# Turning q and k by ordinary products with the identity, placed between the score products of a slot

## The chip, the cores and the metric

The kernel runs on one core of a Trainium2 chip. The metric is device time in microseconds (us). TensorE (PE in the profile) does the matrix products, and its weight loads have records of their own (PEld). VectorE is DVE, ScalarE is ACT, GpSimd is POOL, and SyncE (SP) issues most of the transfers.

## The reference, cut to what matters

Attention over 2 batches, 8 heads, 768 tokens and 64 dimensions per head, then two MLPs over the 1536 tokens. A query sees the keys whose hash agrees with its own: six bits, the signs of products with `proj`.

```python
q_bits = (np.einsum('bhsd,dk->bhsk', q, proj) > 0)
k_bits = (np.einsum('bhsd,dk->bhsk', k, proj) > 0)
mask = q_bucket[:, :, :, None] == k_bucket[:, :, None, :]
scores = np.where(mask, scale * np.matmul(q, k.transpose(0, 1, 3, 2)), -1e9)
attn = np.exp(scores - np.max(scores, axis=-1, keepdims=True))
attn = attn / (np.sum(attn, axis=-1, keepdims=True) + 1e-09)
x = np.matmul(attn, v)                       # heads side by side: 1536 x 512
x = (silu(x @ w_gate) * (x @ w_val)) @ w_out
x = layernorm(solu(x @ w_in)) * g_ln @ w_out2
```

## The kernel before, in words

The attention works on eight pairs of heads. A pair is 12 slots; a slot is 128 queries of one head against all 768 keys. Slots are numbered `i` over the whole stage, and `l` is the slot's place in its pair `p`. Everything is written out by hand inside `manual_schedule()`: each engine runs its instructions in the order in which the loop at L819 issues them.

float32 values are kept as two parts, a rounded high one and the rest, both in the type fp32r (a float32 that TensorE multiplies in one pass). `parts[p, "q"]` and `parts[p, "k"]` hold both parts of a token side by side, 128 values on the free axis. The score products want them with these values on the partitions, so each block of 128 tokens is turned on TensorE: 12 blocks for each head (6 of k, 6 of q), four at a time into one PSUM bank. One such group of four is a *turn* (`turns`, L460): four transposes (L475), the fourth of them with its type read as float32, and after a `yield` one or two ScalarE copies out of the bank (L480; L482 and L483; or L492), and transfers that put the pieces where the scores read them. A head takes three turns, `g` = 0, 1, 2.

A slot issues, in this order:

- DVE takes the row maxima of the slot's scores (`maxima`, L563).
- PE transposes the exponentials of two slots earlier, two groups of three blocks of 128x128 (`transposes`, L597 and L595). In a slot without a turn the last of the six is read as float32 (L595); in a slot with a turn it is not.
- `go(work)` at L836: PE does the four transposes of a turn, if the slot has one (`turning`, L728, says which: l = 0, 1, 3, 9, 10, 11 in most pairs), or hash products (L514) in other slots. In the first pair `beginning` (L756) plays this part, with one or two turns at a time.
- PE computes the scores of the next slot (`scores`, L544): two products with the high parts (`ka`, `qa`) and two with the low parts and hash bits (`kb`, `qb`), each of 384 columns, into one of two score tiles. The tile is that of the slot before, so the first of the four waits for that slot's exponential.
- ACT and DVE take the transposed exponentials out of PSUM (`highs` L606, `lows` L610).
- PE multiplies the values of a head, four products (`values`, L632, L636, L631).
- `go(work)` at L851: the ACT copies of the turn.
- ACT computes the slot's exponential (`exps`, L577), with the row sums read out after it (ACTIVATION_READ_ACCUMULATOR).

After the attention the two MLPs run from L870 on, as products of 512 columns without pause; nothing of them is changed.

Of the kernel before, what the change touches and what calls it, by code (L numbers as in the profile page):

```python
# [10 lines left out]
F32 = mybir.dt.float32  # L11
R32 = mybir.dt.float32r
# [9 lines left out]
P = 128  # L22
# [49 lines left out]
def hash_attention_then_two_mlps(  # L72
# [16 lines left out]
    nc = tc.nc  # L89
# [46 lines left out]
    first = {}  # L136
# [41 lines left out]
    for g in range(4):  # L178
        m = (g + 1) % 2
# [50 lines left out]
    with at:  # L230
# [6 lines left out]
        ps_a = at.enter_context(tc.tile_pool(name="ps_a", bufs=1, space=PSUM))  # L237
        ps_p = at.enter_context(tc.tile_pool(name="ps_p", bufs=1, space=PSUM))
# [68 lines left out]
        def move(dst, src):  # L307
            nc.sync.dma_start(dst.bitcast(F32), src.bitcast(F32))
# [137 lines left out]
        def tiles_of_head():  # L446
            return {
                x: (kp if x == "kt" else ab).tile([P, S], R32, tag=x, name=x)
                for x in ("qa", "qb", "ka", "kb", "kt")
            }  # L450
# [3 lines left out]
        def turn(p, j, g, bank=None):  # L454

            return turns(p, j, g, bank) if p < len(pairs) else iter(())

        def turns(p, j, g, bank):  # L460

            if (p, j) not in turned:
                turned[p, j] = tiles_of_head()
            x = turned[p, j]
            if bank is None:
                t = ps_p.tile([P, 512], R32, tag="pp", name="pp")
            else:
                t = ps_a.tile([P, 512], R32, tag="av", name="av")
            for m in range(4):
                nm, c = ("k", 4 * g + m) if 4 * g + m < C else ("q", 4 * g + m - C)  # L470
                sides = (
                    t[:, m * P:(m + 1) * P],
                    parts[p, nm][:, j, c].rearrange("p t d -> p (t d)"), idr,
                )
                nc.tensor.transpose(*(x.bitcast(F32) if m == 3 else x for x in sides))  # L475
            yield
            t = t.bitcast(F32)
            qa, qb, ka, kb, kt = (x[nm] for nm in ("qa", "qb", "ka", "kb", "kt"))
            if g == 0:
                nc.scalar.mul(kt[:, 0:512], t, qscale)  # L480
            elif g == 1:
                nc.scalar.mul(kt[:, 512:S], t[:, 0:S - 512], qscale)  # L482
                nc.scalar.copy(qa[:, 0:1024 - S], t[:, S - 512:512])  # L483
                move(qb[D:P], kt[0:D])
                keys = [(ka[0:D], kt[0:D]), (ka[D:P], kt[0:D]), (kb[0:D], kt[D:P])]
                if p == 1:
                    held.extend(keys)
                else:
                    for dst, src in keys:
                        move(dst, src)  # L490
            else:
                nc.scalar.copy(qa[:, 1024 - S:S], t)  # L492
                move(qb[0:D], qa[0:D])
                if p == 1 and j == 1:
                    for dst, src in held:
                        move(dst, src)
# [37 lines left out]
        def quarter(h):  # L534


            p, l = divmod(h, 4)
            return (p, l // 2, l % 2) if p == 0 else (p, l % 2, l // 2)
# [2 lines left out]

            return quarter(h)[1] == 1

        def scores(i):  # L544
            if not 0 <= i < NSLOT:
                return
            p, j, n = quarter(i // CH)
            x, c = turned[p, j], n * CH + i % CH
            s = s_tiles[i % 2]
            rows = slice(c * P, (c + 1) * P)  # L550
            for a, m, first in ((x["qa"], x["ka"], True), (x["qb"][:MB], x["kb"][:MB], False)):
                for n in range(2):
                    nc.tensor.matmul(  # L553
                        s[:, n, :HALF], a[:, rows], m[:, n * HALF:(n + 1) * HALF],
                        start=first, stop=not first,
                    )
            s_of[i] = s

        def maxima(i):
# [23 lines left out]
        def transposes(i, g, last=False):  # L583
            if not 0 <= i < NSLOT:
                return
            h, c = divmod(i, CH)
            if c == 0 and g == 0:
                eh_of[h] = et.tile([P, C, HALF], R32, tag="eh", name="eh")
                el_of[h] = et.tile([P, C, HALF], R32, tag="el", name="el")
            t = ps_t.tile([P, CH, P], R32, tag="t", name="t")  # L590
            e, moved = e_of[i]
            for m in range(CH):
                cols = slice(m * P, (m + 1) * P)
                if last and m == CH - 1:
                    nc.tensor.transpose(t.bitcast(F32)[:, m, :], e[:, g, cols], idf)  # L595
                else:
                    nc.tensor.transpose(t[:, m, :], moved[:, g, cols], idr)  # L597
            t_of[i, g] = t.bitcast(F32)
# [5 lines left out]
        def highs(i, g):  # L604
            if 0 <= i < NSLOT:
                nc.scalar.copy(half_tile(eh_of, i, g), t_of[i, g])  # L606
# [115 lines left out]
        def go(work):  # L722

            next(work, None)
# [31 lines left out]
        def beginning(i):  # L756

            at = {
                3: lambda: (turn(1, 0, 0), turn(1, 0, 1, 1)),
                4: lambda: (turn(1, 0, 2), turn(1, 1, 0, 1)),  # L760
                5: lambda: (turn(1, 1, 1),),
                6: lambda: (turn(1, 1, 2),),
                8: lambda: (hashes(1, 0, False),),
                9: lambda: (hashes(1, 1, False),),
                10: lambda: (turn(2, 0, 0),),
                11: lambda: (turn(2, 0, 1),),
            }
            works = at[i]() if i in at else ()
            for work in works:
                go(work)  # L770
            yield
            for work in works:
                go(work)
# [34 lines left out]
        with tc.manual_schedule():  # L808
            for p, nm in ((1, "k"), (1, "q"), (0, "v")):
                load(p, nm)  # L810
            first_weights = early()
            opening = (
                step for of in ((1, "k"), (1, "q"), (0, "v")) for step in split_heads(*of)
            )
            opened = start()
            hashed = next(opened)
            done = leaving = iter(())
            splits = {}
            for i in range(NSLOT + 9):  # L819
                p, l = divmod(i, SLOTS)  # L820
                h, part = divmod(i - 5, CH)
                if i < SLOTS:
                    work = beginning(i)
                else:
                    work = turning(p, l)
                if part == 0:
                    leaving, done = done, results(h - 1)
                    go(done)
                maxima(i)
                if part == 0 and h - 1 >= NQ - 2:  # L830
                    go(done)
                transposes(i - 2, 0)
                if i < 2:
                    go(hashed)
                transposes(i - 2, 1, getattr(work, "__name__", "") != "turns")
                go(work)  # L836
                if i == 2:
                    hashed = first_hashes(1)
                    go(hashed)
                scores(i + 1)  # L840
                if i == 0:
                    go(opened)
                for g in range(2):
                    highs(i - 2, g)
                    lows(i - 2, g)
                if part == 0:
                    go(leaving)
                values(h, part)
                if part == 2 and h == NQ - 1:
                    spread(*quarter(h)[::2])  # L850
                go(work)  # L851
                if i == 2:
                    go(hashed)
                exps(i)
                if i == 0:
                    go(opened)
                if i < 6:
                    for _ in range((2, 1, 3, 2, 2, 1)[i]):
                        go(opening)
                splitting(p, l)  # L860
                go(done if part == 2 else leaving)
                if part == 2 and h == NQ - 2:
                    widen(*quarter(NQ - 1)[::2], "both")
                if part == 1:
                    go(done)
                    sums(h + 1)
                if p > 1 and l in (3, 9, 11):
                    go(first_weights)
# [39 lines left out]
    with ExitStack() as m1:  # L908
# [281 lines left out]
        for t in range(TH):  # L1190
            for unit in range((FT + 1) * NBLK):
# [14 lines left out]
                work = hidden(t * FT + f, blk) if f < FT else summed(t, blk)  # L1206
# [38 lines left out]
    with ExitStack() as m2:  # L1245
# [173 lines left out]
        for p in range(1, tiles // 2):  # L1419
            a, b = 2 * p, 2 * p + 1  # L1420
            x, y, z, w = (bank(n) for n in range(4))
            work = paired(p, x, y, z, w)
# [92 lines left out]
```

## Time and profile before

| | |
|---|---|
| time, median of 3 runs | 668.08 us (667.76 to 668.36) |
| profiled execution, its own time | 668.38 us |
| its span, first to last instruction | 666.6 us |
| PE busy in the span | 659.7 us (99%) |
| DVE, ACT, POOL busy | 80%, 56%, 32% |
| granted TensorE clock | 1.000 of full speed |

The span is what the records of instructions cover; the execution's own time has 1.8 us more around it. The attention takes about the first 238 us of it. Busy shares are averages over stages; PE at 99% says only that it hardly ever stands idle, not that it runs at its peak.

### The profile page before, as it was taken

Reading aid. Unit: us, or ns where it says so; the run is one execution under the profiler, and the core shown is the slowest. Engines: PE = TensorE matmul, PEld = TensorE weight load, DVE = VectorE, ACT = ScalarE, POOL = GpSimd, SP = SyncE. Lnnn points to the kernel's source line nnn. Section 1 sums busy time; section 2 is a strip of 40 time slices with the busy share of each in tenths; the row PEclk is TensorE's granted clock in tenths of the full one; section 3 lists DMA queues with packets and bytes.
Section 4 is the critical chain, followed back from the end, with each engine's and each line's share of the span. In section 5 each row is a group of like instructions: output and inputs, shape, how many; then the busy total and the mean of one; then the engine's idle time right before and its main releaser. Section 6 shows DMA issues by size and latency. Waiting matters only on the chain.

```text
span 666.6 us, 10299 instructions
## 1 busy us (share of the span) xinstructions
PE 659.7 (99%) x3653; PEld 577.4 (87%) x3653; DVE 530.4 (80%) x912; ACT 371.1 (56%) x754; POOL 215.2 (32%) x247
## 2 busy tenths in 40 slices
PE   8999999999999999999999999999999999999998
PEld 6999999999999988888888888888888888888887
DVE  8889899999999978857868968858974979865781
ACT  7898898989989844644235234224143433342432
POOL 6647566666625420000000000000000575776200
PEclk9999999999999999999999999999999999999999
DMA  6684753746434123352132643213014111212201
GB/s 189 178 211 110 198 145 97 193 123 156 110 81 158 31 64 126 131 186 67 60 126 71 223 150 109 82 64 126 1 63 164 70 84 42 85 65 96 94 17 48
DMA packets 39347, 73.19 MB, mean 110 GB/s; under 512 B 5336, under 2 KB 26904, under 8 KB 38528
## 3 DMA queue, kind: packets, MB, share of 16 engines
q1 hardware_dynamic: 39296, 72.53, 35.5%
q8 instruction: 29, 0.48, 0.3%
q14 instruction: 22, 0.18, 0.1%
HBM read 40.90 MB, written 7.34 MB: 72 GB/s over the span
## 4 chain that ended last, share of the span: by engine, by line
PE 95%; DVE 2%; ACT 1%; DMA 0%; issue 0%; SPq 0%; ACTq 0%; DVEq 0%
PE h L1133 29%; PE s L553 9%; PE h L1263 8%; PE t L597 6%; PE y L1161 5%; PE y L1160 5%; PE y L1159 5%; PE av L632 5%; PE av L636 4%; PE o L1379 3%; PE o L1377 3%; PE o L1378 3%; PE pp L514 2%; PE pp L475 2%; PE t L1358 1%; PE t L595 1%
## 5 line engine op out<-in xcount | busy, mean ns | idle before, releaser
L1133 PE MATMUL h<-xh,hi 128*128 128x512 f32 x288 | 112.2, 390 | 0.0
L1133 PE MATMUL h<-xl,hi 128*128 128x512 f32 x288 | 112.1, 389 | 0.0
L1133 PE MATMUL h<-xh,lo 128*128 128x512 f32 x288 | 111.2, 389 | 0.0
L610 DVE SCALAR_TENSOR_TENSOR el<-t,eh 128x384 fp32r<-128x384 f32 x192 | 97.7, 550 | 16.9 <-ACT eh L606 16.0
L606 ACT CAST eh<-t 128x384 fp32r<-128x384 f32 x192 | 84.5, 499 | 19.5 <-PE t L597 18.9
L1089 POOL TENSOR_TENSOR sf<-yh 128x256 f32<-128x256 f32 x5 | 3.7, 736 | 277.7 <-ACT yh L1174 277.7
L563 DVE TENSOR_REDUCE top<-s 128x1 f32<-128x770 f32 x96 | 90.8, 946 | 0.9 <-PE s L553 0.8
L632 PE MATMUL av<-eh,vs 128*128 128x384 f32 x186 | 64.5, 347 | 0.1
L1133 PEld LDWEIGHTS h<-xh,hi 128*128 128x128 f32 x288 | 54.1, 188 | 11.4 <-DVE sg L1143 0.2
L1133 PEld LDWEIGHTS h<-xl,hi 128*128 128x128 f32 x288 | 54.1, 188 | 11.3
L1133 PEld LDWEIGHTS h<-xh,lo 128*128 128x128 f32 x288 | 54.0, 188 | 11.1
L1143 DVE TENSOR_TENSOR sg<-h,sg 128x512 f32<-128x512 f32 x36 | 24.8, 689 | 43.0 <-PE h L1133 23.6
L553 PE MATMUL s<-ka,qa 128*128 128x384 f32 x192 | 55.2, 368 | 1.4 <-ACT e1f L577 1.2
L1062 ACT CAST hi<-wf 128x1024 fp32r<-128x1024 f32 x17 | 17.9, 1050 | 68.9 <-DVE wf L68 56.9
L1159 PE MATMUL y<-ah,hi 128*128 128x512 f32 x144 | 56.0, 389 | 0.0
L1160 PE MATMUL y<-al,hi 128*128 128x512 f32 x144 | 56.0, 389 | 0.0
L1161 PE MATMUL y<-ah,lo 128*128 128x512 f32 x144 | 56.0, 389 | 0.0
L1145 ACT CAST ah<-sg 128x512 fp32r<-128x512 f32 x36 | 22.4, 622 | 59.7 <-DVE sg L1143 59.7
L636 PE MATMUL av<-el,vs 128*128 128x384 f32 x155 | 52.3, 338 | 0.0
L553 PE MATMUL s<-kb,qb 76*128 76x384 f32 x192 | 49.5, 338 | 0.1
L1171 DVE TENSOR_TENSOR yf<-y,yf 128x512 f32<-128x512 f32 x60 | 40.3, 686 | 4.8 <-PE y L1161 4.5
L553 PEld LDWEIGHTS s<-kb,qb 76*128 76x128 f32 x192 | 34.9, 189 | 0.7 <-DMA kb<-bits 0.4
(295 smaller groups left out, 1611.6 us busy)
## 6 DMA issues: line engine op xcount, KB each, us to landing
raw<-in_moe_w_out_dram SPq DMA_DIRECT2D x10, 1024.0 KB
raw<-in_moe_w_gate_dram SPq DMA_DIRECT2D x12, 512.0 KB
raw<-in_moe_w_val_dram SPq DMA_DIRECT2D x12, 512.0 KB
ka<-kt SPq DMA_DIRECT2D x30, 192.0 KB
raw<-in_moe_w_in_dram SPq DMA_DIRECT2D x4, 1024.0 KB
parked<-raw SPq DMA_DIRECT2D x8, 512.0 KB
moved<-u SPq DMA_DIRECT2D x8, 512.0 KB
v<-in_v_dram SPq DMA_DIRECT2D x8, 384.0 KB
```

Of the source, the lines that this page charges most:

```text
L553: nc.tensor.matmul(s[:, n, :HALF], a[:, rows], m[:, n * HALF:(n + 1) * HALF], start=first, stop=not first,)
L563: bias_of[:] = [nc.vector.tensor_reduce(tops[i % len(tops)], s_of[i][:, :, :HALF + 1], AX.XY, ALU.max, negate=True)]
L606: nc.scalar.copy(half_tile(eh_of, i, g), t_of[i, g])
L610: last_of[i] = nc.vector.scalar_tensor_tensor(half_tile(el_of, i, g), t_of.pop((i, g)), EVEN, half_tile(eh_of, i, g).bitcast(F32), ALU.add ...
L632: nc.tensor.matmul(av, vj[:, c], eh_of[h][:, c, :], start=c == 0, stop=c == C - 1)
L636: nc.tensor.matmul(*low, start=False, stop=False)
L1133: nc.tensor.matmul(ps[n], a[:, n, kk, :], x[:, kk, blk * BLK:(blk + 1) * BLK], start=kk == 0 and a is hi and x is xh, stop=kk == KD - 1 an ...
L1159: nc.tensor.matmul(p, hi[:, cols], ah, start=f == t * FT, stop=False)
L1160: nc.tensor.matmul(p, hi[:, cols], al, start=False, stop=False)
L1161: nc.tensor.matmul(p, lo[:, cols], ah, start=False, stop=f == (t + 1) * FT - 1)
L1171: nc.vector.tensor_add(y, p, y)
L1263: nc.tensor.matmul(dst, a[m](d), w3_of[b][:, l, d], start=start and n == 0, stop=n == 3 * KH - 1, skip_group_check=True,)
```

## The change

The four transposes of a turn become four ordinary products (`nc.tensor.matmul`) of the same blocks with the same identity `idr`. Operands and results stay the same values; the PSUM tile is declared float32. None of the four is read as float32 any more. `turns` now yields after each of the four.

In slots whose work is a turn, the four products are no longer issued ahead of the scores. `scores` is handed the generator and takes two steps of it behind the first score product and two behind the second. The last of the six transposes of the exponentials is now read as float32 in every slot. In `beginning` the four products of a turn are still issued together ahead of the scores.

```diff
@@ turns
-                t = ps_p.tile([P, 512], R32, tag="pp", name="pp")
+                t = ps_p.tile([P, 512], F32, tag="pp", name="pp")
...
-                sides = (
+                nc.tensor.matmul(
                     t[:, m * P:(m + 1) * P],
                     parts[p, nm][:, j, c].rearrange("p t d -> p (t d)"), idr,
+                    start=True, stop=True,
                 )
-                nc.tensor.transpose(*(x.bitcast(F32) if m == 3 else x for x in sides))
-            yield
-            t = t.bitcast(F32)
+                yield
@@ scores
-        def scores(i):
+        def scores(i, work=iter(())):
...
+                    if first:
+                        go(work)
+                        go(work)
@@ beginning
-                go(work)
+                for _ in range(4 if work.__name__ == "turns" else 1):
+                    go(work)
@@ the loop over the slots
-                transposes(i - 2, 1, getattr(work, "__name__", "") != "turns")
-                go(work)
+                transposes(i - 2, 1, True)
+                between = getattr(work, "__name__", "") == "turns"
+                if not between:
+                    go(work)
...
-                scores(i + 1)
+                scores(i + 1, work if between else iter(()))
```

What PE has before in a slot with a turn (pair 2, l = 10), from the slot's first transpose to its last score product; `t` is the PSUM tile of the transposed exponentials, `pp` that of the turn, `s_168` a score tile:

```order
L597 MATMUL t<-idr,e1r 128x128 [waits DVE_49]
L597 MATMUL t<-idr,e1r 128x128 x2
L597 MATMUL t<-idr,e1r 128x128 [waits DVE_49]
L597 MATMUL t<-idr,e1r 128x128 x2
L475 MATMUL pp<-idr,ks 128x128 [waits Activation_49]
L475 MATMUL pp<-idr,ks 128x128
L475 MATMUL pp<-idr,qs 128x128 [waits Pool_49]
L475 MATMUL pp<-idr,qs 128x128
L553 MATMUL s_168<-ka,qa 128x384 [waits Activation_49]
L553 MATMUL s_168<-ka,qa 128x384
L553 MATMUL s_168<-kb,qb 128x384 x2
```

The same place on PE in the changed kernel, where the lines of `transposes`, `turns` and `scores` are L599, L597, L471 and L552:

```order
L599 MATMUL t<-idr,e1r 128x128 [waits DVE_49]
L599 MATMUL t<-idr,e1r 128x128 x2
L599 MATMUL t<-idr,e1r 128x128 [waits DVE_49]
L599 MATMUL t<-idr,e1r 128x128
L597 MATMUL t<-idr,e1f 128x128
L552 MATMUL s_168<-ka,qa 128x384 [waits Activation_49]
L471 MATMUL pp<-idr,ks 128x128 [waits PE_49]
L471 MATMUL pp<-idr,ks 128x128
L552 MATMUL s_168<-ka,qa 128x384
L471 MATMUL pp<-idr,qs 128x128 [waits Pool_49]
L471 MATMUL pp<-idr,qs 128x128
L552 MATMUL s_168<-kb,qb 128x384 x2
```

The four blocks of the turn have moved behind the first score product, which waits for ACT; the turn's last block now ends behind the second score product.

On ACT, the same slot and the next one before (`eh` are the casts, `e0f` and `e3f` the exponentials):

```order
L606 CAST eh<-t 128x3x128 [waits PE_49] x2
L482 ACTIVATE kt<-pp 128x256 [waits PE_49]
L483 CAST qa<-pp 128x256 [waits DMAHW2_49]
L577 ACTIVATE e0f,total<-s_167,top_172 128x768 [waits DVE_49,Activation_49]
L703 COPY both<-av 128x384 [waits DMAHW3_49,DMAHW2_49,PE_49]
L606 CAST eh<-t 128x3x128 [waits PE_49,Activation_49]
L606 CAST eh<-t 128x3x128 [waits PE_49]
L492 CAST qa<-pp 128x512 [waits PE_49]
L577 ACTIVATE e3f,total<-s_168,top_173 128x768 [waits DVE_49,Activation_49]
```

And the same in the changed kernel:

```order
L608 CAST eh<-t 128x3x128 [waits PE_49] x2
L481 ACTIVATE kt<-pp 128x256 [waits PE_49]
L482 CAST qa<-pp 128x256 [waits DMAHW2_49]
L579 ACTIVATE e0f,total<-s_167,top_172 128x768 [waits DVE_49,Activation_49]
L705 COPY both<-av 128x384 [waits DMAHW3_49,DMAHW2_49,PE_49]
L608 CAST eh<-t 128x3x128 [waits PE_49,Activation_49]
L608 CAST eh<-t 128x3x128 [waits PE_49]
L491 CAST qa<-pp 128x512 [waits PE_49]
L579 ACTIVATE e3f,total<-s_168,top_173 128x768 [waits DVE_49,Activation_49]
```

Nothing moves on ACT: the copies out of `pp` stand between the casts and the exponential in both.

## Rows read from the trace of the kernel before

**Rows 1.** The page: granted clock by slices, chain that ended last by engine.

```profile
PEclk9999999999999999999999999999999999999999
...
PE 95%; DVE 2%; ACT 1%; DMA 0%; issue 0%; SPq 0%; ACTq 0%; DVEq 0%
```

**Rows 2.** Busy by stretch: length, PE, PEld, DVE, ACT, POOL, PEclk, DMA, GB/s.

```profile
0.00:20.00 20.00, 16.85 (x108) 13.20 (x108) 16.91 (x49) 15.37 (x32) 14.05 (x26) 1.00 0.59 169
...
90.00:120.00 30.00, 30.00 (x228) 29.45 (x226) 28.32 (x51) 27.32 (x66) 20.02 (x18) 1.00 0.57 145
```

**Rows 3.** Chain in order of time, 92.2 to 100 us: start, us, what.

```profile
94.39 0.47 PE t L597 x6
94.87 0.38 PE pp L475 x4
95.25 0.70 PE s L553 x4
...
96.66 0.50 PE t L597 x6
...
98.97 0.38 PE t L597 x5
99.35 0.14 PE t L595
```

**Rows 4.** The turn's line: ns min/median/max, first and last start in us.

```profile
L475 PE MATMUL pp<-idr,qs x82: 227/253/306, 18.4 to 186.3; 128*128 128x128 f32 x82
L475 PE MATMUL pp<-idr,ks x78: 227/252/306, 15.6 to 181.6; 128*128 128x128 f32 x78
L475 PE MATMUL av<-idr,ks x6: 232/268/307, 16.1 to 19.0; 128*128 128x128 f32 x6
L475 PE MATMUL av<-idr,qs x2: 249/274/299, 16.3 to 16.4; 128*128 128x128 f32 x2
```

**Rows 5.** Timeline of PE's weight loads around 95 and 12 us: start, us.

```profile
94.96 0.32 PEld L553 LDWEIGHTS s<-ka,qa 128*128 128x128 f32 x2
...
95.62 0.19 PEld L632 LDWEIGHTS av<-eh,vs 128*128 128x128 f32 x1
...
11.69 0.30 PEld L553 LDWEIGHTS s<-ka,qa 128*128 128x128 f32 x2 [1.12 <-ACT e1f L577]
```

**Rows 6.** Timeline of PE, products of 512 and 256 columns near the end.

```profile
656.27 0.39 PE L1378 MATMUL o<-yx,lh 128*128 128x512 f32 x1
656.50 0.39 PE L1379 MATMUL o<-yx,ll 128*128 128x512 f32 x1
...
658.12 0.28 PE L1377 MATMUL o<-hi,lh 128*128 128x256 f32 x1
658.24 0.28 PE L1378 MATMUL o<-lo,lh 128*128 128x256 f32 x1
```

**Rows 7.** Timeline of ACT, 92.2 to 99.6 us: slots l = 11 and 0.

```profile
93.35 0.66 ACT L492 CAST qa<-pp 128x512 fp32r<-128x512 f32 x1
...
94.63 0.28 ACT L577 ACTIVATION_READ_ACCUMULATOR e3f<-s,top 128x1 f32 x1
...
95.45 0.70 ACT L480 ACTIVATE kt<-pp 128x512 fp32r<-128x512 f32 x1
...
96.72 0.31 ACT L577 ACTIVATION_READ_ACCUMULATOR e1f<-s,top 128x1 f32 x1
```

**Rows 8.** Timeline of all engines, around 21 and 101.5 us.

```profile
20.79 0.22 ACT L577 ACTIVATION_READ_ACCUMULATOR e1f<-s,top 128x1 f32 x1
...
21.06 0.30 PEld L553 LDWEIGHTS s<-ka,qa 128*128 128x128 f32 x2 [0.38 <-ACT e1f L577]
21.06 0.61 PE L553 MATMUL s<-ka,qa 128*128 128x384 f32 x2 [0.19 <-ACT e1f L577]
...
101.13 0.63 PE L597 MATMUL t<-idr,e2r 128*128 128x128 f32 x6
...
101.54 0.86 ACT L606 CAST eh<-t 128x384 fp32r<-128x384 f32 x2 [0.28 <-PE t L597]
```

More of the change, by code (lines that the diff above doesn't have):

```diff
@@ L465, in turns @@
             if bank is None:
-                t = ps_p.tile([P, 512], R32, tag="pp", name="pp")
+                t = ps_p.tile([P, 512], F32, tag="pp", name="pp")
             else:
-                t = ps_a.tile([P, 512], R32, tag="av", name="av")
+                t = ps_a.tile([P, 512], F32, tag="av", name="av")
             for m in range(4):
                 nm, c = ("k", 4 * g + m) if 4 * g + m < C else ("q", 4 * g + m - C)
-                sides = (
+                nc.tensor.matmul(
                     t[:, m * P:(m + 1) * P],
                     parts[p, nm][:, j, c].rearrange("p t d -> p (t d)"), idr,
+                    start=True, stop=True,
                 )
-                nc.tensor.transpose(*(x.bitcast(F32) if m == 3 else x for x in sides))
-            yield
-            t = t.bitcast(F32)
+                yield
             qa, qb, ka, kb, kt = (x[nm] for nm in ("qa", "qb", "ka", "kb", "kt"))
```

## The prediction

> **What bounds the kernel now.** I read four views. The page comes first: the chain that ended last is 95% PE, and the granted clock is full in every slice [rows 1]. Then the busy time by stretches: between 90 and 120 us PE is busy for all of 30 us, but ACT for 27.3 and DVE for 28.3 [rows 2]. So PE sets the pace with little room beside it. Only at the start, 16.85 us busy of 20, does PE wait. Third, the chain in order of time shows what a slot with a turn consists of: 0.47 us of transposed exponentials, 0.38 of turn, 0.70 of scores, and values up to the next slot at 96.66; from 94.39 that is 2.27 us without a gap [rows 3]. Any PE time added there lengthens the run.
>
> The fourth view, the timeline of ACT against PE's weight loads, shows what is close to taking over. The exponential of slot l = 11 has its sums read out at 94.63 + 0.28 = 94.91, and the load for the first score product of the next slot starts at 94.96 [rows 5, 7]. From such a read-out to a load that had been waiting for it is 0.05 us too (20.79 + 0.22 = 21.01 to 21.06 [rows 8]). So at this place the score product starts with no slack at all: PE is full, and ACT has just released it.
>
> **The PE price of a turn.** One transpose more or less is worth 0.47 - 0.38 = 0.09 us, and the one read as float32 takes 0.14 [rows 3]. A slot with a turn loses the turn's 0.38. Its six transposes become five and one of float32: 0.38 + 0.14 = 0.52 in place of 0.47. So 0.33 us go, and four ordinary products of 128 columns come.
>
> None of these stands in the trace, so I bound the spacing c that each brings. Below: 512 columns take 0.23 us from start to start and 256 take 0.12 [rows 6], 0.055 for each 128, which leaves 0.065 where the weight load is hidden. Above: 0.23, if a narrow product costs what a 512-column one does. Between them stands the load of the weights, one for each product. Where two product loads follow each other with nothing ahead, both take 0.30 us and one takes 0.19 [rows 5]: they follow at 0.11. The first turn product has its load beneath the 0.175 of a score product and costs 0.065 behind it; the second waits 0.11 for its load, which can only begin when the first has taken its weights over, and the score product behind it waits 0.11 for its own. Each pair costs 2 x 0.11, as the loads set it. I take c = 0.11, the nearest row, and keep 0.065 and 0.23 as ends. PE then needs -0.33 + 4 x 0.11 = +0.11 us more, 2.38 for a slot. 168 transposes [rows 4] are 42 turns; 8 are issued by `beginning` and 34 by `turning`. 34 x 0.11 = 3.7 us. In `beginning` the products stand in one string, 0.1 us dearer each; PE has idle time there [rows 2], so I count half of 8 x 0.1, 0.4 us.
>
> The Trainium skill, Perfetto Trace Analysis, section Transposes, says that logical transposes should use the transpose and not a standard product, since they skip arithmetic. The rows point the same way, 0.09 against at least 0.11, though through the weight load; the rule gives no price.
>
> **The wait that appears.** The copy of a turn out of PSUM stands on ACT behind the casts and ahead of the slot's exponential, and that order stays. Before, the turn was done before the first score product. Now its last block ends behind the second one, so ACT waits for PE with the exponential queued behind it, and the first score product of the next slot waits for that exponential. Where turns follow in neighbouring slots this is a loop, and its length is the sum of rows:
> - read-out to the load of the first score product: 0.05 [rows 8]
> - load to that product's end: two end at 21.06 + 0.61 = 21.67, the second a score spacing of 0.175 (0.70 / 4) behind the first, so 0.44 [rows 3, 8]
> - to the end of the turn: 0.065 + 0.11 for the first pair, 0.11 + 0.11 until the second score product ends (its load is late by 0.11, and its 384 columns take 0.11 longer than 128), 0.065 + 0.11 for the second pair: 0.57
> - PE's end to ACT's start: six transposes end at 101.76, the third of them three spacings of 0.09 earlier, about 101.50, and the cast that waits for it starts at 101.54: 0.04 [rows 8]
> - copy to read-out of the exponential: 93.35 to 94.91 and 95.45 to 97.03: 1.57 [rows 7]
>
> That is 2.67 us, against 2.38 of PE work: PE waits 0.29 us in the slot behind each turn. It does so where that slot goes straight from the transposes to its scores: in pair 1 behind l = 0, 1, 2, 3, 9, 10, 11 (7), in pairs 2 to 5 behind 0, 1, 9, 10, 11 (20; behind l = 3 stand hash products, which cover it), in pair 6 behind 0 and 1 (2). 29 x 0.29 = 8.4 us. The casts don't hide it: two of them end well before the turn does.
>
> What else moves: the transfers that a copy issues on SP start some 0.3 us later, and their readers come a slot or more later, 2.3 us or more; the hash products and POOL's splits keep their places. I count these at nothing; if the transfers were late, the hash products would wait up to 0.3 us in four pairs, about 1 us. DVE gets longer slots and waits less. The MLPs keep PE busy from their first product, so the attention's delay goes into the time whole.
>
> **Sum.** 3.7 + 0.4 + 8.4 = 12.5 us on the profiled execution's 668.38 (span 666.6 and 1.8 around it), 680.9. That execution is 0.3 above the median of the runs, so I predict 680.6 us.
>
> **Rivals.**
> 1. *PE's price alone.* If ACT's copy is not late enough to reach the next slot's score product, only 3.7 + 0.4 remain: 672.2 us. For it: in hash slots ACT has room. Against it: the score product has no slack already [rows 5, 7], and it moves forward in its slot by the turn's 0.38 while the copy moves back.
> 2. *Loads as quick as in transposes.* With c = 0.085 (a transpose's spacing, 0.09 by rows 3 at most) PE pays nothing: -0.33 + 0.34. The loop is then 0.05 + 0.44 + 0.50 + 0.04 + 1.57 = 2.60 against 2.28, and 29 x 0.32 = 9.3 us remain: 677.5. Against it: two product loads at 0.11 [rows 5]. The Trainium skill, TensorE: Matmul & The Clock Gate, section Back-to-back issue gap, gives 81 ns for pairs of a load and a product of 128 columns, which would be this rival; it gives 131 ns for 512 columns, where this trace has 0.23 us [rows 6], so the trace does not bear it out.
> 3. *A narrow product at the price of a wide one*, c = 0.23: PE pays -0.33 + 0.92 = 0.59 a slot, 2.86. The loop, with four times 0.23 and one 0.175 between, is 3.20. 34 x 0.59 + 29 x 0.34 + half of 8 x 0.6 = 32: about 700 us. Only that no row has 128 columns speaks for it; the fall from 0.23 to 0.12 between 512 and 256 columns speaks against.
> 4. *Faster.* The loads are hidden entirely, c = 0.065: 34 x (-0.33 + 0.26) = -2.4, 666 us. It decides from c below 0.083 (0.33 / 4) on, and only if the loop, 0.05 + 0.44 + 0.435 + 0.04 + 1.57 = 2.54 us even then, falls to 2.27 or less: copy to read-out would have to take 1.30 in place of 1.57, or the score product not wait for that exponential. Rows 7 and 8 speak against both. A gain from the clock there cannot be, since it is full already [rows 1, 2]; the Trainium skill, same page, Part 4: PE-mode transpose, says that transposes don't count as work for the clock gate, and no stretch here shows a clock lost to them.
>
> **How the numbers follow.** Forecast 0.66, with its own range of 676 to 686 (c from 0.10 to 0.13, the loop uncertain by 0.07 us in 29 places); rival 1 0.12; rival 2 0.10; rival 3 0.05; rival 4, with a result near zero, 0.07. From 671.5 to 686.5 about 0.82 is held: rivals 3 and 4 and some tails stay outside. A run can tell about 0.2% (1.3 us) from no change: slower by more 0.93, within it 0.02, faster 0.05.
>
> **What would show it.** Weight loads of the turn's line following at 0.11 us within a pair. ACT idle before the turn's copies, put down to PE and the turn's line, about 0.3 us each. PE idle or a long first score product in slots l = 10, 11, 0, 1 and 2, put down to the exponential on ACT, with starts of such slots about 2.67 us apart; slots with hash products unchanged. PE busy below 30 in the stretch from 90 to 120 us, the clock still full, and the MLPs as long as before. The prediction is wrong if slots with a turn follow at 2.38 (rival 1), if the turn's products stand closer than 0.09 or further than 0.15 apart (rivals 2 and 3), or if a slot with a turn takes 2.27 or less.

## The result and the profile after

The changed kernel takes 677.47 us (median of 4 runs, 677.35 to 677.63). The kernel before, on the same chip, takes 668.07 us (667.76 to 668.36). The ratio is 1.0141 [1.0125, 1.0156]: slower by 9.4 us, where 680.6 was forecast, with 671.5 to 686.5 as range. The profiled execution took 677.63 us, its span 675.9 (666.6 before).

Where the time went is seen first from one line of the MLP. The view groups the instructions of a line: ns min/median/max, then first and last start in us. Before:

```profile
L1133 PE MATMUL h<-xh,hi x288: 387/389/475, 231.7 to 512.6; 128*128 128x512 f32 x144
```

And after:

```profile
L1138 PE MATMUL h<-xh,hi x288: 387/389/475, 240.9 to 521.9; 128*128 128x512 f32 x144
```

The first product starts 9.2 us later, the last 9.3, and one lasts as long as before. So the whole loss arises in the attention, ahead of 241 us, and the MLPs pass it on.

The page of after, granted clock by slices and the chain that ended last by engine:

```profile
PEclk9999999999999999999999999999999999999999
...
PE 97%; DVE 1%; ACT 1%; issue 0%; ACTq 0%; DVEq 0%
```

Busy time by stretch, columns as in [rows 2]:

```profile
0.00:20.00 20.00, 17.21 (x104) 13.61 (x105) 16.85 (x49) 15.13 (x32) 13.87 (x26) 1.00 0.59 167
90.00:120.00 30.00, 29.97 (x214) 28.62 (x213) 26.66 (x49) 26.02 (x61) 18.41 (x17) 1.00 0.52 131
```

The clock is full, as in [rows 1, 2]. Read by busy time alone, PE would seem as much the bound as ever: 29.97 of 30 us. But it does 214 products in the stretch where it did 228, while ACT and DVE have less to do than before. The wait shows in other views. The chain in order of time, in the changed kernel's slots l = 10 and 11 (one slot earlier in the pair than [rows 3]; 91.09 is slot l = 9, which waits for nothing):

```profile
91.09 0.18 PE s L552
...
93.45 0.40 PE s L552
93.85 0.17 PE pp L471 x2
94.02 0.23 PE s L552
94.25 0.17 PE pp L471 x2
94.42 0.40 PE s L552 x2
...
96.05 0.45 PE s L552
```

A first score product takes 0.40 and 0.45 in this chain, and 0.18 where nothing is waited for. ACT's timeline of the same stretch (start, us, what, and in brackets the idle time ahead of it with its releaser) answers to [rows 7]:

```profile
93.16 0.20 ACT L579 ACTIVATION_READ_ACCUMULATOR e2f<-s,top 128x1 f32 x1
...
94.46 0.39 ACT L481 ACTIVATE kt<-pp 128x256 fp32r<-128x256 f32 x1 [0.35 <-PE pp L471]
94.74 0.36 ACT L482 CAST qa<-pp 128x256 fp32r<-128x256 f32 x1
94.99 0.92 ACT L579 ACTIVATE e0f<-s,top 128x768 f32<-128x768 f32 x1
95.79 0.21 ACT L579 ACTIVATION_READ_ACCUMULATOR e0f<-s,top 128x1 f32 x1
...
97.10 0.59 ACT L491 CAST qa<-pp 128x512 fp32r<-128x512 f32 x1
97.59 0.91 ACT L579 ACTIVATE e3f<-s,top 128x768 f32<-128x768 f32 x1
98.38 0.20 ACT L579 ACTIVATION_READ_ACCUMULATOR e3f<-s,top 128x1 f32 x1
```

And PE's weight loads, which answer to [rows 5]:

```profile
93.41 0.19 PEld L552 LDWEIGHTS s<-ka,qa 128*128 128x128 f32 x1
...
96.05 0.19 PEld L552 LDWEIGHTS s<-ka,qa 128*128 128x128 f32 x1 [0.20 <-ACT e0f L579]
96.16 0.37 PEld L471 LDWEIGHTS pp<-idr,qs 128*128 128x128 f32 x2
```

Read these three together, and the loop can be walked through. The sums are read out at 93.16 + 0.20 = 93.36; the load starts at 93.41; the first score product is done at 93.85; the turn's last block at 94.42; the copy, for which ACT stood idle 0.35 us, starts at 94.46; the next sums are read out at 96.00, and the next load starts at 96.05. That is 2.64 us from load to load.

The waits of the attention, us in total, times, longest:

```profile
ACT kt L481 <- PE pp L471: 3.5, 10, 0.4
...
ACT kt L479 <- PE pp L471: 2.9, 10, 0.4
...
ACT qa L491 <- PE pp L471: 1.7, 7, 0.4
...
PEld s L552 <- ACT e0f L579: 1.2, 6, 0.2
```

ACT waits 27 times for the turn, 8.1 us in all; no wait of ACT for the turn was among the same rows before. Where the weight loads behind a turn wait for an exponential, they show at most 0.2 us each time. PE's products show next to none of it, since the record of the transpose ahead still runs.

The slots themselves say the same: from the end of one first score product to the end of the next it is 2.580 to 2.646 us in 29 slots, on average 2.607, and the 29 are those that the prediction named. Two turn slots of `beginning`, whose first score products start at 31.72 and 34.03 us, wait for nothing; their four products stand together ahead of the scores, and they take 2.36 and 2.37, where before they took 2.25 and 2.26. Slots with hash products and no turn take 2.43, as before.

### The profile page after: what moved, and what is told of

Same layout as the page of the kernel before. It is cut to its first block, busy times and chain, and to the rows that moved or that the text cites. A ratio compares the mean times of both kernels' runs of the same rounds, so it can differ in the third digit from the quotient of the medians.

```text
span 675.9 us, 10292 instructions
## 1 busy us (share of the span) xinstructions
PE 669.6 (99%) x3653; PEld 583.5 (86%) x3653; DVE 530.8 (79%) x912; ACT 372.6 (55%) x754; POOL 215.3 (32%) x247
## 4 chain that ended last, share of the span: by engine, by line
PE 97%; DVE 1%; ACT 1%; issue 0%; ACTq 0%; DVEq 0%
PE h L1138 29%; PE s L552 11%; PE h L1268 8%; PE t L599 5%; PE y L1166 5%; PE y L1164 5%; PE y L1165 5%; PE av L634 5%; PE av L638 4%; PE o L1384 3%; PE o L1382 3%; PE o L1383 3%; PE pp L513 2%; PE pp L471 2%; PE t L597 2%; PE t L1363 1%
## 5 line engine op out<-in xcount | busy, mean ns | idle before, releaser
L552 PE MATMUL s<-ka,qa 128*128 128x384 f32 x192 | 62.9, 380 | 1.2 <-ACT e1f L579 1.0
L552 PE MATMUL s<-kb,qb 76*128 76x384 f32 x192 | 51.2, 347 | 0.0
L552 PEld LDWEIGHTS s<-ka,qa 128*128 128x128 f32 x192 | 33.8, 193 | 6.6 <-ACT e0f L579 1.2
```

The costliest lines, as they stand in the source:

```text
L552: nc.tensor.matmul(s[:, n, :HALF], a[:, rows], m[:, n * HALF:(n + 1) * HALF], start=first, stop=not first,)
```

## The experiments

Two theories ran against each other. A is the prediction's loop: what costs is where in the slot the turn ends, since ACT's copy, and behind it the exponential, wait for it. B is the price on PE: ordinary products cost more there than transposes, wherever they stand. Lines are those of the changed kernel unless it is said otherwise.

**The four products ahead of the scores.** The same instructions, with the turn back at its old place.

```
-                if not between:
+                for _ in range(4 if between else 1):
                     go(work)
...
-                scores(i + 1, work if between else iter(()))
+                scores(i + 1)
```

> Ordinary products as in the changed kernel, but all four ahead of the scores, where the transposes stood. Theory A (a part of the loss is the price of the weight loads, the larger part a loop PE - turn's copy on ACT - exponential - next slot's first score product): the turn ends before the first score product again, the loop is gone, only the loads' price stays, 34 x 0.1 us: about 672 us, ACT hardly waits for the turn, and slots with a turn take 2.36 us. Theory B (the products themselves cost it all, wherever they stand): as the changed kernel, 677 us.

Measured: 670.64 us (670.52 to 671.03), 1.0035 [1.0022, 1.0048] of the kernel before. No copy waits any more. The chain:

```profile
95.46 0.38 PE t L599 x5
95.84 0.13 PE t L597
95.97 0.40 PE pp L471 x4
96.37 0.74 PE s L552 x4
```

A slot is 2.375, 0.105 more than 2.27 [rows 3], nearly the 0.11 forecast. In 34 slots this is 3.6 us, but the time rises by 2.2. What is missing is found in the kernel before, in three slots of 2.60 to 2.64 us that don't come back here. Two of them, in its weight loads and in its chain:

```profile
36.59 0.30 PEld L553 LDWEIGHTS s<-kb,qb 76*128 76x128 f32 x2 [0.42 <-DMA kb<-bits]
```

```profile
124.64 0.33 PE t L597 x3
124.97 0.01 issue
124.98 0.46 PE t L597 x3
```

In the first, a score product waited 0.42 us for a transfer; in the second, the chain breaks within the transposes, and 0.79 stands where 0.47 would. The third, at 179.2, is 2.61 long like the second, 2.60. Together they are worth 1.0 us over 2.27, and a longer slot can cover such waits. Most of the other 0.4 lies in slots without a turn, which are 0.36 us shorter in all (the largest 1.92 for 2.12 before); why was not followed up. A holds: without the loop 670.64 stands in place of 677.47, 6.8 us less.

**The four products behind all scores.** The opposite: the turn ends later still.

```
-                scores(i + 1, work if between else iter(()))
+                scores(i + 1)
+                if between:
+                    for _ in range(4):
+                        go(work)
```

> The four products behind the fourth score product of the slot, ahead of the values. PE's own price stays at about 0.1 us a slot. Theory A: the turn ends later still, the loop grows to 0.05 + 0.44 + 0.53 + 0.40 + 0.04 + 1.49 = 2.94 us, 29 x 0.58 us of waits: about 688 us. Theory B: as the changed kernel, 677 us.

Measured: 687.93 us (687.65 to 688.14), 1.0291 [1.0276, 1.0307]. Slots that follow each other with a turn take 2.93 to 3.00. One wait of ACT, the load that it delays in the next slot with the product behind that load, and the busy time by stretch:

```profile
95.50 0.60 ACT L479 ACTIVATE kt<-pp 128x512 fp32r<-128x512 f32 x1 [0.56 <-PE pp L471]
```

```profile
97.03 0.30 PEld L552 LDWEIGHTS s<-ka,qa 128*128 128x128 f32 x2 [0.51 <-ACT e2f L579]
```

```profile
97.03 0.62 PE L552 MATMUL s<-ka,qa 128*128 128x384 f32 x2 [0.32 <-ACT e2f L579]
```

```profile
90.00:120.00 30.00, 28.36 (x201) 26.81 (x200) 24.91 (x44) 24.70 (x58) 17.83 (x16) 1.00 0.51 128
```

The same products on PE, at three places in the slot: 670.6, 677.5, 687.9. B, which has 677 for all three, is out. Of the three, only here, with over half a microsecond of wait in a slot, does PE's busy time clearly fall (28.36, against 30.00 and 29.97).

**Transposes at the changed kernel's place.** What stands between the score products is a transpose again, none of them read as float32.

```
...
-                nc.tensor.matmul(
+                nc.tensor.transpose(
                     t[:, m * P:(m + 1) * P],
                     parts[p, nm][:, j, c].rearrange("p t d -> p (t d)"), idr,
-                    start=True, stop=True,
                 )
...
```

> Transposes again (none read as float32), but two behind each of the first two score products, as the products stand in the changed kernel. Theory A: the price of the loads is nearly gone (two transposes behind a score product 0.06 and 0.07, and the score product behind them some 0.05 late for its load), but the loop stays at about 2.50 us against 2.28 of PE work: 29 x 0.22 us, about 674.5 us, the first score product waits for the exponential. Theory B: with the transposes back it is as before, 668 to 669 us.

Measured: 675.19 us (675.07 to 675.43), 1.0101 [1.0085, 1.0118]. The chain of a slot that waited:

```profile
95.15 0.44 PE s L552
95.59 0.13 PE pp L471 x2
95.72 0.25 PE s L552
95.97 0.13 PE pp L471 x2
96.09 0.43 PE s L552 x2
```

A pair takes 0.13 in place of 0.17, but the score product behind it 0.25 in place of 0.23. From the first score product's end to the turn's end that is 0.07 less, and the loop shortens by as much (2.50 forecast; 2.51 to 2.57 measured, 2.58 to 2.65 in the changed kernel). So the kind of instruction is worth 2.3 us here (677.47 to 675.19; 2.6 if each is taken against the kernel before in its own set of runs), and the place the rest.

**The turn's copy behind the exponential.** The changed kernel, with ACT's order turned round in slots with a turn.

```
-                go(work)
+                if not between:
+                    go(work)
                 exps(i)
+                if between:
+                    go(work)
```

> The changed kernel, with the turn's copy behind the slot's exponential on ACT instead of ahead of it. Theory A: the exponential no longer waits for the turn, the loop is cut, the price of the loads stays: about 672 us, slots 2.37 us. Theory B: as the changed kernel, 677 us, since no product is taken away.

Measured: 672.40 us (671.58 to 672.91), 1.0058 [1.0043, 1.0073]. Most slots with a turn fall to 2.37: the exponential behind the copy was what the score products waited for. A new wait appears where the next user of `pp`, the one PSUM bank for turns and hash products, comes close behind. ACT, and the chain, around 128 us:

```profile
127.61 0.59 ACT L479 ACTIVATE kt<-pp 128x512 fp32r<-128x512 f32 x1
```

```profile
128.18 0.18 PE s L552
128.36 0.33 PE pp L471 x2
128.69 0.23 PE s L552
```

The pair takes 0.33 for 0.17: the copy has read the bank until 128.20. The five slots that have a turn and hash products behind it take 3.06 on average, 2.89 in the changed kernel. There the first hash product starts 0.05 us behind the copy's end; it writes the bank that the copy reads, but it also reads `qa`, which the copy writes, so these five don't tell the two apart. The pair above does: its first load too starts 0.05 us behind the copy (128.25), and it reads nothing that the copy writes. The longest single wait is another one, in pair 1: a hash product stands 0.8 us for the transfer of `qb`, and its slot takes 4.02 for 3.34. The changed kernel comes there 0.9 us later and doesn't wait.

```profile
PEld pp L513 <- DMA qb<-qa: 0.8, 1, 0.8
```

**The same in the kernel before.** If the copy's place cost anything there, it should help there too.

```
-                go(work)
+                late = getattr(work, "__name__", "") == "turns"
+                if not late:
+                    go(work)
...
+                if late:
+                    go(work)
```

> The kernel before (transposes ahead of the scores), with the turn's copy behind the slot's exponential. Theory A (the exponential on ACT's way to the next score product is what a late copy holds up): the exponential comes some 0.5 us earlier, the few places where the kernel before waits for ACT go, at most 1 us: 667.3 to 668.4 us. Rival: the copy now ends some 0.5 us after the exponential, which is about where the next slot's transposes want the one PSUM bank again; PE waits there up to 0.1 us in 29 slots, 669 to 671 us.

Measured: 671.76 us (671.69 to 671.99), 1.0051 [1.0039, 1.0063]. The rival was right, and by more than it said. Its ACT and its chain (lines of the kernel before):

```profile
97.72 0.59 ACT L480 ACTIVATE kt<-pp 128x512 fp32r<-128x512 f32 x1
```

```profile
98.00 0.46 PE t L597 x6
98.46 0.49 PE pp L475 x4
```

The turn takes 0.49 for 0.38, since its bank is read until 98.31. So ACT's copy has two deadlines: the exponential behind it, and the next use of the bank.

**Transposes between, copy last.** Both edits at once.

> Transposes between the score products, with the turn's copy behind the exponential. Theory A: the loop is cut, and what is left is the score products' late loads behind the transposes, some 0.05 us in 34 slots: 670 us, slots 2.32 us. Theory B (the place between the score products costs by itself, whatever ACT does): as with the copy ahead of the exponential, 675 us.

Measured: 671.97 us (671.07 to 672.65), 1.0053 [1.0040, 1.0067]. Some slots reach 2.31, as A said, but those ahead of hash products take 3.17 on average, where with the copy ahead of the exponential they took 2.84. As in the run with the ordinary products and the copy last, the first hash product starts 0.05 us behind the copy, held by the bank or by `qa`. That takes back much of what the loop gave up; 670 was too hopeful by 2 us.

**The last transposed exponential.** The first experiment's order, with the sixth transpose of a turn slot read as the other five are.

```
-                transposes(i - 2, 1, True)
+                transposes(i - 2, 1, getattr(work, "__name__", "") != "turns")
```

> All four products ahead of the scores (as in the run with them there), and the last transpose of the exponentials in a slot with a turn not read as float32, as in the kernel before. If the float32 reading costs what its spacing says, 0.05 us in 34 slots, about 669 us. If the first product's weight load has to wait for the transposes in either case, the spacing only moves from the transpose to the product: 670.6 us.

Measured: 671.69 us (671.33 to 672.53), 1.0052 [1.0040, 1.0064]. Neither expectation holds: it is no faster, and about 1 us slower than the first experiment, with intervals that just overlap. Its chain:

```profile
93.35 0.46 PE t L599 x6
93.81 0.47 PE pp L471 x4
94.28 0.75 PE s L552 x4
```

The turn takes 0.47 behind such a transpose and 0.40 behind the one read as float32. So that transpose is no price of the change: its 0.05 come back in the products behind it.

**The turn first in its slot.** The kernel before, with the turn ahead of the transposed exponentials on PE and its copy ahead of the casts on ACT, to get past both deadlines. The reading as float32 goes from the turn's last block to the sixth exponential.

```
+                if early_turn:
+                    go(work)
...
-                go(work)
+                if not early_turn:
+                    go(work)
```

> The kernel before with the turn (transposes, as before) at the head of its slot on PE, ahead of the transposed exponentials, and its copy ahead of the casts on ACT: the other way from the change. If ACT's copy is what stands between PE and the next score product, the copy now runs while ACT would wait for PE, the exponential starts 0.05 to 0.1 us earlier, and the places where the kernel before waits for ACT (about 1 us in all) go: 667.2 to 668.0 us. If those places come from DVE, whose work on the casts now starts 0.4 us later, nothing is gained or PE waits for it: 668.3 to 669.5 us.

Measured: 676.19 us (676.03 to 676.58), 1.0114 [1.0097, 1.0131]. Both expectations fail, by 6.7 us or more. Some slots also hold a *spread*, three transposes into `pp` (L666) whose result a multiplication on DVE reads from there. Where a turn follows one, a slot takes 3.06 to 3.13, 2.59 to 2.61 before. The weight loads show why (lines of this kernel):

```profile
119.25 0.39 PEld L476 LDWEIGHTS pp<-idr,ks 128*128 128x128 f32 x4 [0.59 <-DVE xf L715]
```

Ten times the turn waits, up to 0.6 us, for a multiplication on DVE that reads the same bank: about 5 of the 7.9 us by the lengths of these slots, and the rest was not traced. I had counted ACT's copies as the bank's only readers.

None of these versions beats the kernel before. A second bank for the turns was not tried.

## Why the prediction was right, and where its sizes were off

*Direction and mechanism.* Both held. The forecast had two terms, the price on PE and the wait; the first experiment gives the first alone (+2.2), and the rest of the 9.4, about 7 us, is the second. The experiment with the turn behind the scores makes the same wait longer and the time with it.

*The price on PE.* The mechanism was the load, as forecast. In the row "96.16 0.37 ... x2" above the first of two loads of 0.19 starts 0.11 behind the score product's; the second starts at 96.16 + 0.37 - 0.19 = 96.34, when the first product begins, and the score product's next load follows 0.11 behind it. I had named 0.11 as the spacing within the pair, and as the sign to look for; it is that of the loads around it, and the pair's own is 0.18. The products' ends are as forecast: the chain has 0.17 for a pair, and 0.23 for the score product behind it, 0.05 more than its usual 0.18. Without a wait a turn slot with its products between the scores takes 2.37 (the run with the copy behind the exponential), 0.10 more than 2.27 and not 0.11. My sign for rivals 2 and 3, products closer than 0.09 or further than 0.15 apart, did not say of what: within a pair the ends stand 0.11 apart, the starts 0.06.

*The loop.* Four of its five terms stand in the rows after as they were forecast: 0.05, 0.44, 0.57 and 0.04. The fifth, copy to read-out, was taken at 1.57 from [rows 7]; in the loop it is 1.48 (97.10 to 98.58), and 1.54 where two copies split the bank (94.46 to 96.00). In [rows 7] ACT had work queued; here it mostly starts from idle (27 waits; at 97.10 the cast ahead of the copy has all but ended), and the copy's record is 0.59 for 0.66 and 0.70. Why the same instructions last less then was not tested. So the loop is 2.607 on average and not 2.67: 29 x 0.06 = 1.8 us.

*Waits that went.* About 1.0 us was the kernel before's own waits, in the three long slots shown above. I had read stretches in which PE is full and had not asked what a longer slot would cover.

*The rest.* 1.8 + 1.0 explain 2.8 of the 3.1 us by which 680.6 lay too high. The price, 0.01 less in each of the five of the 34 slots that don't wait, is under 0.1 of what is left, and the remainder was not traced. For `beginning` 0.4 us was allowed: PE's busy time in the first 20 us rose by 0.36 (16.85 to 17.21), but what of that reached the time was not measured by itself. Hash slots kept their 2.43, so the transfers, which were counted at nothing, were not late here.

*A sign that hardly showed.* I wrote that PE's busy time would fall below 30 in the stretch from 90 to 120 us. It is 29.97, which nobody would read as a wait. A wait of 0.24 us (a slot of 2.61 with 2.37 of work) fits within the records of the products around it, which overlap: a transpose read as float32 starts at 95.75, and its record of 0.30 ends where the delayed product and its load begin.

```profile
95.75 0.30 PE L597 MATMUL t<-idr,e2f 128*128 128x128 f32 x1
96.05 0.45 PE L552 MATMUL s<-ka,qa 128*128 128x384 f32 x1
```

The count of products in the stretch, 214 for 228, was the sign to name.

*The rivals.* Price alone (672.2) was excluded by 29 slots of 2.6 us; the four products at the turn's old place, without the wait, took 670.6. Quicker loads (677.5) hit the measured time and the loop (2.60) better than my forecast did, but by luck: it had no price on PE, and a slot without a wait is not 2.28 but 2.37; loads follow at 0.11 around a pair and not at 0.085, and what shortened the loop was the path from copy to read-out.

## What to carry to other kernels

Where two engines pass work to each other in order, an instruction's place decides when the other engine's next one is freed: sum the path around the loop, with the queue behind the waiting instruction in it, before moving anything later. Look for the other deadlines as well, above all who else uses the buffer: all four versions here that moved the copy behind the exponential, or the turn to the head of its slot, had waits at the one bank. And count products in a stretch: where records overlap, busy time does not show waits shorter than a record.

## What the hardware showed beyond this

- The spacing of narrow instructions depends on their neighbours. Behind six plain transposes four 128-column products and their start take 0.47 us, behind one read as float32 0.40; a score product behind two transposes takes 0.25, behind two products 0.23, behind another score product 0.18.
- A wait of 0.51 us on a weight load shows as 0.32 on the product behind it, and a wait of 0.24 us leaves PE's busy share at 29.97 of 30.
